# Queries and keys of eight token tiles by seven half products a pair, with low parts and softmax steps moved to Pool

## The chip, the cores and the metric

The kernel runs on one core of a Trainium2 chip. The metric is the device time of one execution, in microseconds. The engines that matter are PE (TensorE), DVE (VectorE), ACT (ScalarE), POOL (GpSimd) and the DMA queues that SP and ACT issue to. Each engine takes its own instructions in order and waits on semaphores for the others.

## The reference

With S = 2048 tokens of width D = 512, 32 heads of 16, and F = 1792:

```python
xn = layernorm(x)                                  # no weights
q, k, v = split_heads(xn @ wqkv)                   # [512, 1536]
kg, vg = k, v at positions s - 2*j, j = 0..7       # dilated sliding window
logits = sum(q * kg, -1) * 16 ** -0.5              # masked where s - 2*j < 0
o = sum(softmax(logits) * vg); s = merge_heads(o) @ wo
h = relu(xn @ w1 + b1) ** 2
g = silu(h @ w2 + b2)
out = x + s * g
```

All is float32.

## The kernel before

**Products.** A float32 factor is kept as a high part (rounded to the matmul's format by an ACT copy, `high`) and a low part (the rest, by a subtraction, `low`), and a product is made of three passes, high by high, high by low and low by high (`PASSES`). A product of 128 tokens by 512 columns with 512 summed over is so 4 slices (kt) by 3 passes, 12 matmuls of 128x512.

**First stage.** The 16 tiles of 128 tokens (t) are taken in pairs a, b = a + 1. For each tile there is a product q, k and v (`qkv(t, s)`, s = 0, 1, 2; `pq` in the profile). Its result lies in one of four PSUM banks (`psA`, tag "acc"), which are taken in turn; ACT copies it to `stg` (`evacuate`), and each pair's stg goes to DRAM (sq, sk, sv), from where attention loads its own layout. In the same stage, ahead by two pairs, a tile is normalised: from tile 6 on ACT sums the row (`mean`, tile scratch) and Pool scales the sum; ACT sums the squares (`spread`) and Pool makes the inverse deviation (`rs`: scale, then power) and `shift`; ACT writes `xn` (`norm`). A pair's xn goes through DMAs (`shuffle`, to `xb`), DVE transposes it (`trans`, to `pxT`), ACT copies the high part (`xt`) and DVE subtracts the low one (`lowx`).

**Second stage.** For four chunks c of 512 tokens, and f = 0 to 13: `up` makes 128 rows of h in PSUM (`ph`), ACT applies relu and squares, DVE subtracts the low part (`lowh`); `down` adds h times w2 into four banks `pb`. The output products of attention (`pw`) are put between them. The weights w1 and w2 are split in the same way (`w`), the first two by DVE, the others by Pool.

**Attention.** 8 units of 256 tokens run on DVE beside all that: four multiplications k by q of 128x2048 (`pr`) with their reductions to L, softmax steps on L (subtract the maximum, exp on ACT, multiply by the inverse sum), four multiplications by v (`pv`) with their reductions.

**What sets the order.** Each engine's instructions stand in the order in which the program's Python issues them: the helper `Ordered` records each one, so most have its line, L80 (L84 in the changed kernel). Only attention is placed by a planner: `pump` draws attention's next step whenever the sum of DVE's estimated durations lies behind PE's. So the order of calls in the loop over pairs is the order of each engine. Names in the order views carry a running number at their end, such as `pq2_0_399`: product 0 (q) of tile 2; `DMA` rows are loads and stores issued by that engine.

## Time and profile before

| | us |
|---|---|
| median of 3 runs | 496.63 (496.25 to 498.05) |
| the profiled execution | 495.58 |
| its span | 493.8 |
| PE busy | 487.5 (99%) |
| DVE busy | 431.7 (87%) |
| ACT busy | 211.0 (43%) |
| POOL busy | 97.9 (20%) |

The span is the stretch that the profiler shows; the execution's own time has 1.78 us more around it. Rows of a timeline read: start and duration in us, engine, line, operation, written tile <- read tiles, how many, and in brackets how long the engine had stood idle, and what released it. Rows of groups give the busy time, the mean duration in ns, and the idle time before them. The windows view gives, for each stretch, the busy time of each engine with its instructions, then the granted clock of PE, the share of the DMA engines and GB/s.

### The profile page before, as it was taken

What the parts mean: (1) busy time and instruction counts of PE and PEld (TensorE: products, weight loads), DVE (VectorE), ACT (ScalarE), POOL (GpSimd) and SP (SyncE); (2) the same over time, 40 slices, a digit from 0 to 9 for tenths busy, and PEclk for the clock granted to TensorE, in tenths of its full rate; (3) what the DMA queues carried; (4) which work ended last, traced back from release to release, by engine and by line L of the source; (5) the groups of instructions that cost most, each with busy time, mean ns of one, the idle gap of its engine ahead of it and who ended that gap; (6) DMA issues with size and microseconds to landing.
All of it is one profiled execution on the core that took longest, in us unless ns stands there. A gap on an engine that the chain in (4) does not pass through costs nothing.

```text
span 493.8 us, 5860 instructions
## 1 busy us (share of the span) xinstructions
PE 487.5 (99%) x2154; PEld 401.1 (81%) x2154; DVE 431.7 (87%) x370; ACT 211.0 (43%) x377; POOL 97.9 (20%) x105
## 2 busy tenths in 40 slices
PE   8999999999999999999999999999999999999997
PEld 5888888888888888887888888888888888888886
DVE  5925798998999999998999998899999889999445
ACT  5636455563343665316333324432252354313331
POOL 1311015571000779300112000112100011220000
PEclk9999999999999999999999999999999999999999
DMA  7999979769977892653406408043241805030222
GB/s 287 297 287 341 304 238 313 225 238 323 372 228 262 203 274 65 202 212 118 127 31 216 181 22 329 4 164 123 85 161 43 328 2 202 1 127 1 85 85 86
DMA packets 48520, 88.79 MB, mean 180 GB/s; under 512 B 5372, under 2 KB 32364, under 8 KB 45676
## 3 DMA queue, kind: packets, MB, share of 16 engines
q1 hardware_dynamic: 44172, 54.87, 35.3%
q10 hardware_dynamic: 4320, 33.56, 19.1%
q8 instruction: 17, 0.28, 0.2%
q14 instruction: 11, 0.09, 0.1%
HBM read 57.94 MB, written 27.32 MB: 173 GB/s over the span
## 4 chain that ended last, share of the span: by engine, by line
PE 83%; DVE 9%; issue 4%; ACT 2%; DMA 1%; ACTq 0%; POOL 0%; DVEq 0%; POOLq 0%
PE pq L80 27%; PE ph L80 24%; PE pb L80 24%; PE pw L80 8%; DVE v L80 2%; DVE pr L80 2%; DVE h L80 2%; DVE pv L80 1%; DMA x<-in_A_x 1%; ACT ph L80 0%; DVE sm_None L80 0%; ACT z L80 0%; DVE z L80 0%; ACT h L80 0%; PE pxT L80 0%
## 5 line engine op out<-in xcount | busy, mean ns | idle before, releaser
L80 PE MATMUL pb<-w,h 128*128 128x512 f32 x672 | 160.6, 389 | 0.0
L80 PEld LDWEIGHTS pb<-w,h 128*128 128x128 f32 x672 | 126.1, 188 | 26.2
L80 PE MATMUL ph<-xU,w 128*128 128x512 f32 x504 | 120.7, 389 | 0.3 <-DVE h L80 0.3
L80 PEld LDWEIGHTS ph<-xU,w 128*128 128x128 f32 x504 | 94.6, 188 | 20.2 <-DVE h L80 0.7
L80 ACT ACTIVATE ph<-ph,b1t 128x512 f32<-128x512 f32 x56 | 37.0, 661 | 163.0 <-PE ph L80 158.4
L80 PE MATMUL pq<-wq,xt 128*128 128x512 f32 x432 | 98.7, 390 | 0.0
L80 PEld LDWEIGHTS pq<-wq,xt 128*128 128x128 f32 x432 | 81.0, 188 | 17.2 <-ACT stg L80 0.3
L80 DVE TENSOR_TENSOR pr<-k,q 128x2048 f32<-128x2048 f32 x32 | 75.4, 2356 | 0.3
L80 DVE TENSOR_TENSOR pv<-v,L 128x2048 f32<-128x2048 f32 x32 | 73.8, 2305 | 0.4
L80 DVE TENSOR_REDUCE L<-pr 128x128 f32<-128x2048 f32 x32 | 72.9, 2279 | 0.6
L80 DVE TENSOR_REDUCE v<-pv 128x256 f32<-128x2048 f32 x32 | 72.9, 2279 | 0.6
L80 POOL TENSOR_TENSOR z<-z,xr 128x512 f32<-128x512 f32 x12 | 23.2, 1936 | 214.7 <-DVE z L80 209.9
L80 DVE TENSOR_TENSOR h<-ph,h 128x512 fp32r<-128x512 f32 x56 | 38.3, 683 | 19.9 <-ACT ph L80 19.9
L80 PE MATMUL pw<-wot,oT 128*128 128x512 f32 (+1 forms) x204 | 45.9, 376 | 0.0
L80 PEld LDWEIGHTS pw<-wot,oT 128*128 128x128 f32 x204 | 36.8, 188 | 7.1
L80 PE MATMUL ph<-xT,w 128*128 128x512 f32 x168 | 40.7, 391 | 0.0
L80 ACT ACTIVATE stg<-pq 128x512 f32<-128x512 f32 x48 | 27.2, 595 | 26.4 <-PE pq L80 16.9
L80 PEld LDWEIGHTS ph<-xT,w 128*128 128x128 f32 x168 | 31.5, 188 | 7.0 <-DVE h L80 0.4
L80 ACT ACTIVATE h<-ph 128x512 fp32r<-128x512 f32 x56 | 33.7, 601 | 1.8
L80 ACT ACTIVATE ph<-ph 128x512 f32<-128x512 f32 x56 | 33.3, 595 | 0.0
L80 PE MATMUL pq<-wq,xT 128*128 128x512 f32 x132 | 31.7, 398 | 0.0
L80 POOL TENSOR_TENSOR w<-w1r,w 128x512 fp32r<-128x512 f32 x12 | 18.9, 1577 | 57.1 <-DMA rwo<-in_A_wo 48.8
(66 smaller groups left out, 309.9 us busy)
## 6 DMA issues: line engine op xcount, KB each, us to landing
k<-sk ACTq DMA_DIRECT2D x8, 1408.0 KB, 8.1
v<-sv ACTq DMA_DIRECT2D x8, 1408.0 KB, 8.3
sx<-xt SPq DMA_DIRECT2D x12, 512.0 KB, 5.5
xU<-sx ACTq DMA_DIRECT2D x6, 1024.0 KB, 5.4
x<-in_A_x SPq DMA_DIRECT2D x16, 256.0 KB, 5.0
sk<-stg SPq DMA_DIRECT2D x8, 512.0 KB, 7.1
sq<-stg SPq DMA_DIRECT2D x8, 512.0 KB, 5.6
q<-sq ACTq DMA_DIRECT2D x8, 512.0 KB, 8.4
```

The costliest lines, as they stand in the source:

```text
L80: return tc.keep_in_program_order(f(*a, **k))
```

## The change

**Seven half products.** For the pairs 4, 6, 8 and 10, q and k of the two tiles are one 2 by 2 block product: the blocks are the two tiles by the two halves of the 512 summed over, and q and k by the same halves. `pair_of_seven` makes it from seven products of 6 matmuls (`pm<a>_<n>`) in place of four of 12, a form of Strassen's scheme: some factors are sums. Four sums of weight halves (T1 to T4) replace the raw weights at the start of the pairs (DVE in place, ACT the high and Pool the low parts, into `wq6` to `wq9`). Four sums of transposed x, 128 by 256 each (`Sf`, highs and lows in `S<a>_0`, `S<a>_1`), are made in each pair for the next (`sums`, `low_sums`); the low part of `S<a>_1` is Pool's. ACT copies the products 1 and 5, DVE adds the other five to the half-made results in `stg`, and Pool makes two more additions. v stays as it was.

**Places of the normalisation.** `mean`, `spread` and `norm` of a pair start half a pair earlier: mean(a + 6) and spread(a + 6) stand around v of tile a + 1, and the first norm stands at the start of the next pair.

**Weights.** wq lies in ten buffers; the later w buffers w1 to w10 take their places as they come free (`HOME`). The loads and splits of w come later: w0 is split at the end of pair 4, w1 and w2 at the end of pair 12, w3 and w4 at the end of pair 14, then one in each of the first chunk's steps; Pool makes all their low parts.

**Softmax.** For the units 1 to 7 the subtraction of the maximum and the multiplication by the inverse sum are Pool's. The factor 0.25 moves from q's copy into the exponential.

**Low part of h.** From the second chunk on ACT writes the full square to SBUF (`hf`, one buffer) and Pool subtracts.

```diff
+SEVEN = range(4, 12, 2)
...
-            V.tensor_sub(L, L, mx[:, :, None].to_broadcast([P, n, W]))
+            (G if h is None else V).tensor_sub(L, L, mx[:, :, None].to_broadcast([P, n, W]))
...
-                A.activation(L, L, AF.Exp)
+                A.activation(L, L, AF.Exp, scale=0.25)
...
-            V.tensor_mul(L, L, sm[:, :, None].to_broadcast([P, n, W]))
+            (G if h is None else V).tensor_mul(L, L, sm[:, :, None].to_broadcast([P, n, W]))
...
+    def next_w():
+        f = len(w12)
+        if f < NF:
+            w12[f] = buffer(f"w{f}", HOME[f]) if f in HOME else p2.tile([P, 2, 2, 512], FR, name=f"w{f}")
+            for i, r in enumerate(raws.pop(f)):
+                split(w12[f][:, 0, i], w12[f][:, 1, i], r, G)
+            if f + 2 < NF:
+                load_w(f + 2)
...
+    def sums(a, half):
+        (pa, pb), n = (pTs[t].rearrange("p (h m) -> p h m", h=2) for t in (a, a + 1)), 2 * half
+        if half == 0:
+            Sf[a] = hpool.tile([P, 4, 2 * P], F32, name=f"Sf{a}", tag="h", bufs=3)
+            A.activation(Sf[a][:, 3], pb[:, 0], AF.Copy)
+            not_before(seen[a + 1])
+            V.tensor_add(Sf[a][:, 0], Sf[a][:, 3], pb[:, 1])
+            V.tensor_sub(Sf[a][:, 1], Sf[a][:, 0], pa[:, 0])
+        else:
+            V.tensor_sub(Sf[a][:, 2], pa[:, 0], Sf[a][:, 3])
+            V.tensor_sub(Sf[a][:, 3], pa[:, 1], Sf[a][:, 1])
+        Sp[a, half] = hpool.tile([P, 2, 2, 2, P], FR, name=f"S{a}_{half}", tag="h", bufs=3)
...
+        A.activation(Sp[a, half][:, 0].rearrange("p j k n -> p (j k n)"),
+                     Sf[a][:, n:n + 2].rearrange("p j m -> p (j m)"), AF.Copy)
+    def low_sums(a, half, eng):
...
+        eng.tensor_sub(Sp[a, half][:, 1].rearrange("p j k n -> p (j k n)"),
+                       Sf[a][:, n:n + 2].rearrange("p j m -> p (j m)"),
+                       Sp[a, half][:, 0].rearrange("p j k n -> p (j k n)").bitcast(F32))
...
+    def product(a, n, lhs, w):
+        ps = psA(f"pm{a}_{n}")
+        k = 0
+        for i in range(2):
+            for p, q in PASSES:
+                PE.matmul(ps, lhs(p, i), wq[w][:, q, i, :], start=k == 0, stop=k == 5)
+                k += 1
...
-        A.activation(ph, ph, AF.Square)
+        full = hpool.tile([P, 512], F32, name=f"hf{c}_{f}", tag="hf") if c else ph
+        A.activation(full, ph, AF.Square)
+        if c:
+            G.tensor_sub(h[:, 1], full, h[:, 0].bitcast(F32))
...
     shuffle(4)
-    split_w(0, V)
+    for d, x0, x1 in (((0, 0), (1, 0), (0, 0)), ((1, 0), (1, 2), (1, 0)),
+                      ((1, 2), (1, 2), (0, 0)), ((0, 2), (0, 2), (1, 2))):
+        for i in range(2):
+            V.tensor_sub(*(raws[s, kt + i] for s, kt in (d, x0, x1)))
+    for w, (s, kt) in ((T1, (0, 0)), (T2, (1, 2)), (T3, (1, 0)), (T4, (0, 2))):
+        for i in range(2):
+            split(wq[w][:, 0, i], wq[w][:, 1, i], raws[s, kt + i], G)
     pump(LATE)
+    mean(6)
     qkv(1, 2)
-    split_w(1, V)
+    spread(6)
+    mean(7)
     pump(LATE)
...
+    def pair_of_seven(a):
...
+        if ahead:
+            norm(a + 4)
+            spread(b + 4)
+        p = product(a, 1, part_x(a, 0), Q0)
+        A.activation(q[:, :, 0], p, AF.Copy)
+        p = product(a, 5, part_s(a, 0), T1)
+        A.activation(k[:, :, 1], p, AF.Copy)
+        pump(LATE)
+        if ahead:
+            norm(b + 4)
+            shuffle(a + 4)
+        p = product(a, 6, part_s(a, 1), T2)
+        not_before(clock["PE"])
+        V.tensor_add(k[:, :, 0], q[:, :, 0], p)
+        p = product(a, 2, part_x(a, 1), Q1)
+        pump(LATE)
+        not_before(clock["PE"])
+        V.tensor_add(q[:, :, 0], q[:, :, 0], p)
+        p = product(a, 7, part_s(a, 2), T3)
+        pump(0)
+        not_before(clock["PE"])
+        V.tensor_add(q[:, :, 1], k[:, :, 0], p)
+        G.tensor_add(k[:, :, 0], k[:, :, 0], k[:, :, 1])
+        G.tensor_add(k[:, :, 1], k[:, :, 1], q[:, :, 1])
+        qkv(a, 2)
+        trans(a + 2)
+        trans(b + 2)
+        if seven:
+            sums(a + 2, 0)
+        pump(LATE)
+        p = product(a, 3, part_s(a, 3), K1)
+        lowx(a + 2)
+        pump(LATE)
+        not_before(clock["PE"])
+        V.tensor_add(k[:, :, 0], k[:, :, 0], p)
+        store_qkv(b, 1)
+        p = product(a, 4, part_x(b, 1), T4)
+        if seven:
+            low_sums(a + 2, 0, V)
+            sums(a + 2, 1)
+        pump(LATE)
+        not_before(clock["PE"])
+        V.tensor_add(q[:, :, 1], q[:, :, 1], p)
+        store_qkv(b, 0)
+        lowx(b + 2)
+        if seven:
+            low_sums(a + 2, 1, G)
...
+    NEXT = {4: 1, 12: 2, 14: 2}
+    for a in range(2, NT, 2):
...
+        (pair_of_seven if a in SEVEN else pair)(a)
+        if a == 2:
+            load_w(0)
+            load_w(1)
+        for n in range(NEXT.get(a, 0)):
+            next_w()
+        if a + 6 < NT:
+            mean(a + 6)
+        pump(LATE)
+        qkv(a + 1, 2)
+        if a + 6 < NT:
+            spread(a + 6)
+            mean(a + 7)
```

**Where instructions move.** POOL at the start of the pairs, before (the powers of tiles 4 and 5, then tiles 6 and 7):

```order
L80 TENSOR_TENSOR rs4_329<-rs4_329,mhalf_136 128x1
L80 TENSOR_TENSOR rs5_336<-rs5_336,mhalf_136 128x1
L80 TENSOR_SCALAR mean6_395<-mean6_395 128x1
L80 TENSOR_SCALAR rs6_414<-rs6_414 128x1
L80 TENSOR_TENSOR rs6_414<-rs6_414,mhalf_136 128x1
L80 TENSOR_TENSOR shift6_415<-mean6_395,rs6_414 128x1
L80 TENSOR_SCALAR mean7_421<-mean7_421 128x1
```

and in the changed kernel, where `wq6` to `wq9` hold T1 to T4:

```order
L84 TENSOR_TENSOR rs4_326<-rs4_326,mhalf_143 128x1
L84 TENSOR_TENSOR rs5_333<-rs5_333,mhalf_143 128x1
L84 TENSOR_TENSOR wq6_117<-wqraw0_133,wq6_117 128x512 x2
L84 TENSOR_TENSOR wq7_118<-wqraw1_2_129,wq7_118 128x512
L84 TENSOR_TENSOR wq7_118<-wqraw1_3_131,wq7_118 128x512
L84 TENSOR_TENSOR wq8_119<-wqraw1_0_123,wq8_119 128x512
L84 TENSOR_TENSOR wq8_119<-wqraw1_1_127,wq8_119 128x512
L84 TENSOR_TENSOR wq9_120<-wqraw0_133,wq9_120 128x512 x2
L84 TENSOR_SCALAR mean6_390<-mean6_390 128x1
L84 TENSOR_SCALAR rs6_409<-rs6_409 128x1
L84 TENSOR_TENSOR rs6_409<-rs6_409,mhalf_143 128x1
L84 TENSOR_TENSOR shift6_410<-mean6_390,rs6_409 128x1
```

The eight low parts of the combined weights stand between the powers of tiles 4 and 5 and the mean of tile 6.

ACT around the copy of q of tile 2 (`stg2_0<-pq2_0`), before:

```order
L80 ACTIVATE scratch6_396,mean6_395<-x6_236 128x512
L80 ACTIVATE stg2_0_412<-pq2_0_399 128x4x128
L80 ACTIVATE scratch6_416,rs6_414<-x6_236,mean6_395 128x512
L80 ACTIVATE scratch7_422,mean7_421<-x7_297 128x512
L80 ACTIVATE stg2_0_412<-pq3_0_425 128x4x128
L80 ACTIVATE xt4_440<-pxT4_441 128x512
L80 ACTIVATE xn6_444<-x6_236,shift6_415,rs6_414 128x4x4x32
L80 ACTIVATE scratch7_450,rs7_448<-x7_297,mean7_421 128x512
L80 ACTIVATE stg2_1_468<-pq2_1_455 128x4x128
```

and changed:

```order
L84 ACTIVATE scratch6_391,mean6_390<-x6_243 128x512
L84 ACTIVATE stg0_2_350<-pq1_2_394 128x4x128
L84 ACTIVATE scratch6_411,rs6_409<-x6_243,mean6_390 128x512
L84 ACTIVATE scratch7_417,mean7_416<-x7_294 128x512
L84 DMA q0_420<-sq_147 128x1x1024
L84 ACTIVATE xn6_423<-x6_243,shift6_410,rs6_409 128x4x4x32
L84 ACTIVATE scratch7_429,rs7_427<-x7_294,mean7_416 128x512
L84 ACTIVATE stg2_0_447<-pq2_0_434 128x4x128
L84 ACTIVATE xn6_423<-x7_294,shift7_428,rs7_427 128x4x4x32
L84 ACTIVATE stg2_0_447<-pq3_0_457 128x4x128
```

The copy of q of tile 2 stood behind the first sum of tile 6; now it stands behind the squares of tiles 6 and 7 and the first norm, and the copy of q of tile 3 behind the second norm.

PE in pair 6, before:

```order
L80 MATMUL pq6_0_684<-wq0_111,xt6_579 128x512 x12
L80 MATMUL pq7_0_713<-wq0_111,xt7_612 128x512 x12
L80 MATMUL pq6_1_748<-wq1_112,xt6_579 128x512 x12
L80 MATMUL pq7_1_776<-wq1_112,xt7_612 128x512 x12
L80 MATMUL pq6_2_805<-wq2_113,xt6_579 128x512 x12
L80 MATMUL pq7_2_824<-wq2_113,xt7_612 128x512 x12
```

and changed, up to the first product of pair 8:

```order
L84 MATMUL pm6_1_756<-wq0_111,xt6_662 128x512 x6
L84 MATMUL pm6_5_764<-wq6_117,S6_0_674 128x512 x6
L84 MATMUL pm6_6_782<-wq7_118,S6_0_674 128x512 x6
L84 MATMUL pm6_2_790<-wq1_112,xt6_662 128x512 x6
L84 MATMUL pm6_7_799<-wq8_119,S6_1_696 128x512 x6
L84 MATMUL pq6_2_809<-wq4_115,xt6_662 128x512 x6
L84 MATMUL pq6_2_809<-wq5_116,xt6_662 128x512 x6
L84 MATMUL pm6_3_838<-wq3_114,S6_1_696 128x512 x6
L84 MATMUL pm6_4_848<-wq9_120,xt7_666 128x512 x6
L84 MATMUL pq7_2_868<-wq4_115,xt7_666 128x512 x6
L84 MATMUL pq7_2_868<-wq5_116,xt7_666 128x512 x6
L84 MATMUL pm8_1_911<-wq0_111,xt8_824 128x512 x6
```

Four products of q and k have become seven of 6 matmuls; the products 1, 5, 6 and 2 stand ahead of product 7, and v of tile 6 stands between 7 and 3. In the changed kernel a whole product is shown as two rows of 6.

More of the change, by code (lines that the diff above doesn't have):

```diff
@@ L119, in split @@
         low(hi, lo, src, eng)
-    ident = const.tile([P, P], F32, name="ident")
+    p1ctx = ExitStack()
+    px, pstg, pxT = (p1ctx.enter_context(tc.tile_pool(name=n, bufs=1)) for n in ("px", "pstg", "pxT"))
+    xins = {}
+    ident = px.tile([P, P], F32, name="ident")
     make_identity(nc, ident)
@@ L138, in load_x, with buffer @@
         dma(xins[t], tile_rows(x, t))
-    wq = [pwq.tile([P, 2, KT, 512], FR, name=f"wq{s}") for s in range(3)]
+    def buffer(name, i):
+        return wts.tile([P, 2, 2, 512], FR, name=name, tag=f"b{i}")
+    wq = [buffer(f"wq{i}", i) for i in range(10)]
     raws = {}
@@ L564, in body @@
     constants()
-    for f in range(2):
-        load_w(keep, f)
     qkv(0, 0, lambda: highs(2, 0))
@@ L642, in body @@
         if a == NT - 4:
             dma(b1t, b1.rearrange("(f p) -> p f", p=P))
[L644 to L647 removed]
+        pump(LATE if a + 2 < NT else -SLACK)
     lowh(1)
```

145 lines of the change are left out of this document (69 added, 76 removed).

## The prediction

> **What bounds the kernel now.** I read the page first: the busy table and the chain that ended last.
>
> ```profile
> span 493.8 us, 5860 instructions
> PE 487.5 (99%) x2154; PEld 401.1 (81%) x2154; DVE 431.7 (87%) x370; ACT 211.0 (43%) x377; POOL 97.9 (20%) x105
> PE 83%; DVE 9%; issue 4%; ACT 2%; DMA 1%; ACTq 0%; POOL 0%; DVEq 0%; POOLq 0%
> ```
>
> PE is busy 99% of the span, and its products are the chain. Next, the chain's pieces in order of time, and the idle columns of the groups:
>
> ```profile
> 20.12 112.45 PE pq L80 x492
> 470.92 5.44 PE pw L80 x24
> L80 PE MATMUL pq<-wq,xt 128*128 128x512 f32 x432 | 98.7, 390 | 0.0
> L80 ACT ACTIVATE stg<-pq 128x512 f32<-128x512 f32 x48 | 27.2, 595 | 26.4 <-PE pq L80 16.9 <-DVE L L80 8.2 <-DMA xb<-xn 1.4
> ```
>
> In the q, k, v stage PE runs 492 matmuls without a gap: 112.45/492 = 0.2286 us each, 2.743 us for a product of 12. It never waited for a copy out of PSUM, although ACT, which makes those copies in its program order, sometimes stood for a long time. Four banks hide it: a product may be copied up to three products late, 3 x 2.743 = 8.23 us after its end. ACT, around 30 to 40 us (start, duration, instruction, idle before):
>
> ```profile
> 28.59 0.60 ACT L80 ACTIVATE stg<-pq 128x512 f32<-128x512 f32 x1 [0.56 <-PE pq L80]
> ...
> 29.69 0.20 ACT L80 ACTIVATION_READ_ACCUMULATOR scratch<-x,mean 128x1 f32 x1
> ...
> 31.40 0.60 ACT L80 ACTIVATE stg<-pq 128x512 f32<-128x512 f32 x1 [0.76 <-PE pq L80]
> 38.14 0.60 ACT L80 ACTIVATE xt<-pxT 128x512 fp32r<-128x512 f32 x1 [6.14 <-DVE pxT L80]
> 38.63 0.81 ACT L80 ACTIVATE xn<-x,shift,rs 128x512 f32<-128x512 f32 x1
> 39.34 0.71 ACT L80 ACTIVATE scratch<-x,mean 128x512 f32<-128x512 f32 x1
> 39.95 0.19 ACT L80 ACTIVATION_READ_ACCUMULATOR scratch<-x,mean 128x1 f32 x1
> 40.05 0.58 ACT L80 ACTIVATE stg<-pq 128x512 f32<-128x512 f32 x1
> ```
>
> The copy at 40.05 is of k of tile 2, which PE had ended at 33.84 (20.12 + 5 x 2.743); it stood behind a transpose that ACT waited 6.14 us for, and cost nothing, since its bank was wanted at 42.07. So the question is whether the changed orders stay inside that slack.
>
> **The gain.** Each of the four pairs takes 42 matmuls for q and k instead of 48: 24 x 0.2286 = 5.5 us, the only work that leaves PE. A pair becomes 66 matmuls, 15.09 us, instead of 72, 16.46 us. But the new products are of 6 matmuls, 1.37 us, and three of them give a copy only 4.1 us of slack instead of 8.2.
>
> **The first wait: the combined weights on Pool.** Eight DVE differences, eight ACT highs and eight Pool lows now stand ahead of tile 6's mean on Pool; behind that mean, on ACT, stand the spreads of tiles 6 and 7, tile 6's norm, and behind them the copy of q of tile 2. That copy frees the bank for v of tile 2, due to start at 20.12 + 6 x 2.743 = 36.58. The rows of now:
>
> ```profile
> 24.90 0.69 DVE L80 TENSOR_TENSOR w<-w1r,w 128x512 fp32r<-128x512 f32 x1
> 25.50 0.69 DVE L80 TENSOR_TENSOR w<-w2r,w 128x512 fp32r<-128x512 f32 x1
> ...
> 28.11 0.23 POOL L80 TENSOR_SCALAR mean<-mean 128x1 f32<-128x1 f32 x1 [3.71 <-ACT scratch L80]
> 29.97 0.19 POOL L80 TENSOR_SCALAR rs<-rs 128x1 f32<-128x1 f32 x1 [1.63 <-ACT scratch L80]
> 30.24 0.57 POOL L80 TENSOR_TENSOR rs<-rs,mhalf 128x1 f32<-128x1 f32 x1
> 30.89 0.19 POOL L80 TENSOR_TENSOR shift<-mean,rs 128x1 f32<-128x1 f32 x1
> ```
>
> The differences start where DVE split w0 before, 24.90, 0.61 us apart. One difference (to 25.6) and one high (0.62) put the first low at 26.3. What a low costs on Pool:
>
> ```profile
> 94.69 1.29 POOL L80 TENSOR_TENSOR w<-w1r,w 128x512 fp32r<-128x512 f32 x1 [1.93 <-ACT w L80]
> 94.89 3.24 DVE L80 TENSOR_TENSOR pr<-k,q 128x2048 f32<-128x2048 f32 x1
> 95.94 3.35 POOL L80 TENSOR_TENSOR w<-w2r,w 128x512 fp32r<-128x512 f32 x1
> 98.17 2.29 DVE L80 TENSOR_REDUCE L<-pr 128x128 f32<-128x2048 f32 x1
> 100.49 2.29 DVE L80 TENSOR_TENSOR pr<-k,q 128x2048 f32<-128x2048 f32 x1
> 100.69 2.53 POOL L80 TENSOR_TENSOR rs<-rs,mhalf 128x1 f32<-128x1 f32 x1
> ```
>
> A low alone takes 1.25 (94.69 to 95.94). The next one lay under DVE's big multiplication and took 3.35: it ended 1.16 after that did. The multiplication itself was 0.95 over its usual 2.29, about as long as the first low still had to run. Likewise a power of 128x1, 0.57 alone, took 2.53. So a Pool operation and a DVE operation of two SBUF inputs run one after the other, either way. The differences are such operations. Eight lows: 26.3 + 8 x 1.25 = 36.4; with some 5.6 differences still to come, x 0.61 = 3.4: 39.8. Behind them mean 0.2, spread 0.9 with its read, rs, power and shift 1.2 (29.97 to 31.08), norm 0.71 and spread 0.71 (38.63 to 40.05), copy 0.6: 44.2. Waited: 44.2 - 36.58 = **7.6 us**; without the turns 4.2. [...]
>
> **Pair 4.** Its sums of transposed halves follow in a row. From PE's resuming at s: the end of tile 7's power chain on Pool 0.65, norm 0.71, two copies 1.1, four steps of transposing and splitting tile 4 and 5 (0.6 to 0.7 each) 2.55, a half copy and two sums of 128x256 1.25, high and low of the first sums 1.3, two differences and a high 1.5: s + 9.0 in all, some of it overlapping, I take 8.5. Then Pool's low of the second sums 1.25, and tile 8's mean, spread, rs with power and shift (a power under DVE's first multiplication, +0.7), norm, the spread of tile 9, and the copy of product 1: 0.25 + 0.95 + 1.85 + 0.75 + 0.7 + 0.6 = 5.1, so s + 15.0. PE wants that bank for product 7, the fifth in its order, after 48 matmuls, s + 10.97: **4.0 us** (3.3 without turns). For the small pieces the nearest row is this, with the transposes and the splits:
>
> ```profile
> 490.15 0.42 DVE L80 TENSOR_TENSOR z<-z,pw 128x256 f32<-128x256 f32 x1 [0.48 <-PE pw L80]
> ...
> L80 DVE STREAM_TRANSPOSE pxT<-xb 128x512 f32<-128x512 f32 x12 | 8.6, 718 | 18.6 <-DMA xb<-xn 18.6
> L80 DVE TENSOR_TENSOR xt<-pxT,xt 128x512 fp32r<-128x512 f32 x12 | 8.2, 680 | 2.4 <-ACT xt L80 2.4
> ```
>
> **Pairs 6, 8, 10.** From here each pair is a ring of waits from one copy of product 1 to the next. DVE's add to k's first half 0.7, the multiplication's reduction that stands next in DVE's order 2.25, two adds 1.2, both transposes and ACT's half copy 2.35, two sums 0.9, split, add and the first low 1.9, two differences 0.8, ACT's high 0.65, Pool's low 1.3, mean 0.25, spread 0.95, rs to shift 1.15, norm 0.8, spread 0.7, copy 0.55: 16.45 us, against PE's 15.09. In pair 6 w0's two lows stand on Pool ahead of tile 10's mean, +2.5, and one of them meets a DVE multiplication, +2.3: 21.25, a wait of **6.2**. Pair 8: a power under a multiplication, +2.1: 18.55, **3.5**. Pair 10: a softmax step on DVE in the ring, +0.85: 17.3, **2.2**. Without turns 3.9, 1.4 and 1.4; if every handover is 0.1 shorter than I took it, pairs 8 and 10 wait for nothing.
>
> **What I take at nothing.** Low parts of h, softmax steps, and the w buffers:
>
> ```profile
> L80 DVE TENSOR_TENSOR h<-ph,h 128x512 fp32r<-128x512 f32 x56 | 38.3, 683 | 19.9 <-ACT ph L80 19.9
> L80 POOL TENSOR_TENSOR z<-z,xr 128x512 f32<-128x512 f32 x12 | 23.2, 1936 | 214.7 <-DVE z L80 209.9
> L80 DVE TENSOR_TENSOR L<-L,mx_None 128x512 f32<-128x512 f32 x7 | 5.7, 812 | 0.2
> L80 DVE TENSOR_TENSOR L<-L,sm_None 128x512 f32<-128x512 f32 x7 | 5.6, 800 | 0.2
> 261.48 2.72 PE ph L80 x12
> 458.26 2.28 DVE L80 TENSOR_REDUCE v<-pv 128x256 f32<-128x2048 f32 x1
> 467.33 0.69 DVE L80 TENSOR_TENSOR h<-ph,h 128x512 fp32r<-128x512 f32 x1 [4.75 <-ACT ph L80]
> ```
>
> DVE loses 42 x 0.683 = 28.7 and 7 x 1.61 = 11.3 us, 40.0. Its order shows the attention 9 big multiplications with their reductions behind at the end of the first chunk (17 and 12 done there before, now 12 and 8), 9 x 4.6 = 41 by the rows above. So it ends about where it did, 460.5 plus the stalls, while the last out products at 470.92 move by the same stalls: 10 us of cover, taken at 0. A low of h on Pool takes 1.3 to 3.4 and is wanted two steps, four products of 2.72 or 10.9 us, later: 0, at worst 4 if the one full-square buffer holds ACT once or twice. The later w loads in the first chunk wait behind Pool's split two steps ahead: 0, up to 1.7. The q scale moved into the exponential adds no instruction.
>
> **Sum.** The profiled run took 495.58, of which 493.8 is the span: 495.58 - 5.5 + 7.6 + 4.0 + 6.2 + 3.5 + 2.2 = 513.6. The median of the runs shown, 496.63, is 1.05 above the profiled one: 514.6, say 514.5.
>
> **Rivals.**
> *The turns do not count here.* Then the waits are 4.2 + 3.3 + 3.9 + 1.4 + 1.4 = 14.2, and the time 505. For it: my rows show 128x2048 multiplications against Pool, none a 128x512 difference. Against it: a 128x1 power was held as long.
> *The other side: the banks take it all up.* If ACT's copies come in time everywhere, all of the gain stays: 495.58 - 5.5 + 1.05 = 491.1, faster. The place is Pool's mean of tile 6: it must be done by 36.58 - 4.2 = 32.4, which asks that eight lows take 6.1 us, 0.76 each. For it: PE has never waited for a copy in this stage. Against it: no low in the rows is under 1.25.
> *About even.* Only the first wait without turns, 4.2, the later rings just inside PE's pace: 495.58 - 5.5 + 4.2 + 1.05 = 495.3.
> *PE's clock falls in the gaps.* The last slice shows that the granted clock can fall when PE stands:
>
> ```profile
> 490.00:492.00 2.00, 0.11 (x1) 0.00 (x0) 0.84 (x2) 0.00 (x0) 0.00 (x0) 1.00 0.40 140
> 492.00:493.80 1.80, 0.00 (x0) 0.00 (x0) 0.00 (x0) 0.00 (x0) 0.00 (x0) 0.56 0.17 56
> ```
>
> If a product ran at 0.56 after a gap, 2.743 us would be 4.90: 2.15 more. In the rings the copy of product 1 would not come later for it, so the next wait would be shorter by as much; only the last gap's 2.15 is left, 516.7. Where DVE's adds wait for the slower products the ring grows too: up to three gaps more, 2.15 each, 523. Against it: the row falls where the program ends. [...]
>
> **How the numbers follow.** Forecast 0.58 (its own range 507 to 520), no turns 0.13, lower clock 0.10, other side 0.12, about even 0.07. The predicted time is the forecast's, 514.5. The range leaves out the other side and the even case, 0.19: from 498 (the first two waits at their low ends, 7.5, and none later: 498.6) to 522 (the lower clock, most of its gaps not taken up). A measurement of this kernel tells about 0.5% from no change: faster is the other side, 0.12; within 0.5% the even case, 0.07; slower the rest, 0.81.
>
> **What would show it.** Right: PE idle before v of tile 2 at about 36.6, for 4 to 8 us, released by ACT's stg; on Pool eight lows from 26 to 36 or 40 and then the mean; in the four pairs of seven, PE idle ahead of product 7, once a pair, largest in pair 6; no idle time of PE after 140 that was not there. Wrong: PE unbroken from 20 to 127, or lows well under 1.25; or new waits in the chunks, on the full-square buffer or the w loads, or in the attention's end.

## The result

The changed kernel takes 524.37 us (median of 4 runs, 523.89 to 525.79), the kernel before beside it 497.34: a ratio of 1.0549, with a 95% interval of 1.0515 to 1.0583. It is slower, as forecast, but by 27 us where 17 were forecast, and above the end of the range (522).

The page of the changed kernel, busy times, granted clock and chain:

```profile
span 522.1 us, 5929 instructions
PE 492.6 (94%) x2130; PEld 401.6 (77%) x2130; DVE 429.6 (82%) x358; ACT 217.9 (42%) x389; POOL 213.7 (41%) x185
PEclk9996997998999999999999999999999999999999
PE 65%; POOL 10%; issue 10%; ACT 5%; DVE 5%; DMA 3%; SPq 0%; POOLq 0%; ACTq 0%; DVEq 0%
```

PE has 24 matmuls less and yet is busy 5.1 us longer, and it now stands still for 6% of the span; Pool is in the chain with 10%. PEclk shows three dips early in the span. PE's waits, in all, times and the longest:

```profile
PE pm L84 <- ACT stg L84: 13.0, 4, 5.2
PE pq L84 <- ACT stg L84: 7.5, 1, 7.5
PE ph L84 <- DVE h L84: 3.4, 3, 1.7
```

Where they are, from PE's timeline:

```profile
43.91 8.33 PE L84 MATMUL pq<-wq,xT 128*128 128x512 f32 x24 [7.50 <-ACT stg L84]
...
60.01 1.66 PE L84 MATMUL pm<-wq,S 128*128 128x512 f32 x6 [2.20 <-ACT stg L84]
...
80.84 2.93 PE L84 MATMUL pm<-wq,S 128*128 128x512 f32 x6 [5.23 <-ACT stg L84]
83.57 4.50 PE L84 MATMUL pq<-wq,xt 128*128 128x512 f32 x12
...
102.06 1.66 PE L84 MATMUL pm<-wq,S 128*128 128x512 f32 x6 [2.83 <-ACT stg L84]
...
120.42 2.36 PE L84 MATMUL pm<-wq,S 128*128 128x512 f32 x6 [2.73 <-ACT stg L84]
...
129.06 28.16 PE L84 MATMUL pq<-wq,xt 128*128 128x512 f32 x120
157.06 2.93 PE L84 MATMUL ph<-xT,w 128*128 128x512 f32 x12
```

The five waits stand where the prediction put them: ahead of v of tile 2, and ahead of product 7 of each pair, all released by ACT's copy to stg. Behind three of them the rows are too long for their matmuls: 24 in 8.17 us (43.91 to the next product at 52.08), where the 120 undisturbed ones take 28.0, 0.2333 each, which would be 5.6. The windows of the changed kernel (busy times of PE, PEld, DVE, ACT and POOL, then PE's granted clock) show why:

```profile
36.00:38.00 2.00, 0.41 (x2) 0.00 (x0) 0.00 (x0) 0.00 (x0) 2.00 (x2) 1.00 0.74 215
38.00:40.00 2.00, 0.00 (x0) 0.00 (x0) 0.00 (x0) 0.17 (x1) 1.79 (x3) 0.80 1.01 268
40.00:42.00 2.00, 0.00 (x0) 0.00 (x0) 0.00 (x0) 1.50 (x5) 1.12 (x4) 0.50 0.54 190
...
48.00:50.00 2.00, 2.00 (x7) 1.59 (x6) 0.84 (x2) 1.06 (x3) 0.00 (x0) 0.64 1.09 181
50.00:52.00 2.00, 2.00 (x10) 1.65 (x9) 1.71 (x4) 1.04 (x3) 0.00 (x0) 1.00 1.11 342
```

The granted clock falls to half in the gap (at 39.2: a share of (1 - 0.80)/0.5 of the second window is low) and is back only at 49.4, five microseconds after PE resumes. The same happens in pair 6 and pair 10; the windows of all three are in the last section.

The pitch, the time from one matmul's start to the next, changed too. Rows of PE in the first stage, before and changed:

```profile
19.87 22.73 PE L80 MATMUL pq<-wq,xT 128*128 128x512 f32 x96
42.44 90.13 PE L80 MATMUL pq<-wq,xt 128*128 128x512 f32 x396
132.41 2.94 PE L80 MATMUL ph<-xT,w 128*128 128x512 f32 x12
...
19.82 16.59 PE L84 MATMUL pq<-wq,xT 128*128 128x512 f32 x72
```

A row's length holds some 0.16 us more than its matmuls' pitch, because the next product starts that much before the last matmul ends (129.06 + 28.16 = 157.22, and the next starts at 157.06). From start to start, the matmuls of tiles 0 to 3 (`xT`) took 22.57/96 = 0.2351 us each before and 16.43/72 = 0.2282 in the changed kernel; those of the later tiles (`xt`) took 89.97/396 = 0.2272 before and 0.2333 now. So the 0.2286 of the prediction is a mean of two pitches, and the two have changed places.

The whole, by PE's end (490.11 before, 518.38 after, +28.3):

| term | forecast | measured |
|---|---|---|
| 24 matmuls fewer, x 0.2286 | -5.5 | -5.5 |
| five waits | +23.5 (7.6, 4.0, 6.2, 3.5, 2.2) | +20.5 (7.5, 2.2, 5.2, 2.8, 2.7) |
| half clock behind three of them | 0 | +7.1 (2.6, 2.9, 1.6) |
| waits for h (3.4, all in the first chunk; 0.3 before) | 0 | +3.1 |
| pitch: shorter for tiles 0 to 3, longer for the later ones, together | 0 | +2.0 |
| overlap of two products lost at each wait, 0.16 x (8 waits - 1 before) | 0 | +1.1 |

### The profile page after: what moved, and what is told of

Its sections match the earlier page's. It is cut to its first block, busy times and chain, and to the rows that moved or that the text cites. A ratio compares the mean times of both kernels' runs of the same rounds, so it can differ in the third digit from the quotient of the medians.

```text
span 522.1 us, 5929 instructions
## 1 busy us (share of the span) xinstructions
PE 492.6 (94%) x2130; PEld 401.6 (77%) x2130; DVE 429.6 (82%) x358; ACT 217.9 (42%) x389; POOL 213.7 (41%) x185
## 4 chain that ended last, share of the span: by engine, by line
PE 65%; POOL 10%; issue 10%; ACT 5%; DVE 5%; DMA 3%; SPq 0%; POOLq 0%; ACTq 0%; DVEq 0%
PE pb L84 26%; PE ph L84 25%; PE pw L84 8%; PE pq L84 4%; POOL w L84 3%; POOL wq L84 2%; POOL rs L84 2%; ACT scratch L84 1%; POOL S L84 1%; PE pm L84 1%; DMA w2r<-in_B_w 1%; DVE pr L84 1%; DVE Sf L84 1%; DMA sv<-stg 1%; ACT stg L84 1%
## 5 line engine op out<-in xcount | busy, mean ns | idle before, releaser
L84 POOL TENSOR_TENSOR h<-hf,h 128x512 fp32r<-128x512 f32 x42 | 66.9, 1593 | 154.7 <-ACT hf L84 143.8
L84 DVE TENSOR_TENSOR pv<-v,L 128x2048 f32<-128x2048 f32 x32 | 77.2, 2414 | 6.3 <-POOL L L84 5.8
L84 DVE TENSOR_TENSOR pr<-k,q 128x2048 f32<-128x2048 f32 x32 | 80.2, 2507 | 0.5
L84 PE MATMUL pq<-wq,xt 128*128 128x512 f32 x240 | 60.0, 407 | 0.0
L84 PEld LDWEIGHTS pq<-wq,xt 128*128 128x128 f32 x240 | 47.2, 197 | 11.7
L84 PE MATMUL ph<-xT,w 128*128 128x512 f32 x168 | 40.9, 392 | 3.4 <-DVE h L84 3.4
L84 POOL TENSOR_TENSOR w<-w1r,w 128x512 fp32r<-128x512 f32 x14 | 27.6, 1969 | 33.6 <-ACT w L84 33.6
L84 PE MATMUL pq<-wq,xT 128*128 128x512 f32 x132 | 33.7, 416 | 7.5 <-ACT stg L84 7.5
L84 PE MATMUL pm<-wq,S 128*128 128x512 f32 x96 | 26.5, 422 | 13.0 <-ACT stg L84 13.0
L84 PEld LDWEIGHTS pq<-wq,xT 128*128 128x128 f32 x132 | 26.3, 202 | 14.3 <-ACT stg L84 7.9
L84 ACT ACTIVATE stg<-pq 128x512 f32<-128x512 f32 x32 | 19.0, 593 | 43.6 <-PE pq L84 41.6
```

The lines of the kernel that those rows point to most:

```text
L84: return tc.keep_in_program_order(f(*a, **k))
```

## The experiments

The median of the kernel before lay between 497.3 and 499.3 us from one set of runs to the next, so kernels are compared by their ratios to the kernel before beside them: 1.0549 is the change. The changed kernel was not run again beside its edits. By the plain medians most of the gains below are 1 to 3 us smaller than by the ratios, and a difference of that size is not shown.

### The lows of the combined weights on DVE

```diff
-            split(wq[w][:, 0, i], wq[w][:, 1, i], raws[s, kt + i], G)
+            split(wq[w][:, 0, i], wq[w][:, 1, i], raws[s, kt + i], V)
```

> The eight low parts of the combined weights are made by DVE instead of Pool; nothing else differs from the change. My theory (Pool's order holds tile 6's mean behind the eight lows): the mean runs near 32 instead of 39.5, the copy of q of tile 2 ends near 36.2 instead of 43.9, PE's first gap of 7.5 us goes, and with it the low clock after it (2.7 us of PE's time); the wait of pair 4 grows from 2.2 to up to 4, since PE comes there earlier. Time about 516 (514 to 519). Rival, ACT's own order of sums and norms holds the copy: the gap stays over 3 us and the time over 520.

Measured: 1.0383 (1.0350 to 1.0415), 8.3 us less than the change (5.6 by the medians). The first gap falls from 7.5 to 2.37 and no low clock follows it; pair 4's wait grows from 2.2 to 4.4 in two pieces. So the lows on Pool were the cause, and the rival falls. That 2.37 was left has its own reason; POOL of this kernel:

```profile
32.13 2.67 POOL L84 TENSOR_SCALAR mean<-mean 128x1 f32<-128x1 f32 x1 [7.64 <-ACT scratch L84]
```

and DVE:

```profile
29.80 4.90 DVE L84 TENSOR_TENSOR wq<-wqraw,wq 128x512 fp32r<-128x512 f32 x8
```

A mean of 128x1 that took 0.23 before takes 2.67: it ends at 34.80, when DVE's run of eight subtractions ends (34.70). In the change it was the lows that were shut out; DVE:

```profile
24.84 4.90 DVE L84 TENSOR_TENSOR wqraw<-wqraw,wqraw 128x512 f32<-128x512 f32 x8
```

and POOL:

```profile
26.27 13.31 POOL L84 TENSOR_TENSOR wq<-wqraw,wq 128x512 fp32r<-128x512 f32 x8 [1.93 <-ACT wq L84]
39.52 0.28 POOL L84 TENSOR_SCALAR mean<-mean 128x1 f32<-128x1 f32 x1
```

Eight lows take 13.31, 3.3 more than 8 x 1.25: the first of them took 4.63, from 26.27 to 30.90, and DVE's eight differences were through at 29.74. This is the term with turns of the prediction (mean after 39.8, measured 39.52).

### The copies of products 1 and 5 first

```diff
-        if ahead:
-            norm(a + 4)
-            spread(b + 4)
         p = product(a, 1, part_x(a, 0), Q0)
         A.activation(q[:, :, 0], p, AF.Copy)
         p = product(a, 5, part_s(a, 0), T1)
         A.activation(k[:, :, 1], p, AF.Copy)
+        if ahead:
+            norm(a + 4)
+            spread(b + 4)
```

> In the pairs of seven the ACT copies of products 1 and 5 stand ahead of the norm and the spread instead of behind them; nothing else differs from the change. My theory (each pair is a ring through ACT's order): about 2.1 to 2.6 us leave each ring; the wait at product 7 falls from 2.2, 5.2, 2.8, 2.7 to about 0, 3, 0.5 and 0.5; the first gap of 7.5 stays. Time about 514 (511 to 518). Rival, the norms that now come later hold the shuffled x back: DVE's transposes wait for it and the gaps only move: 521 or more.

Measured: 1.0240 (1.0210 to 1.0271), 15 us less than the change (12.9 by the medians; 511.5, near the fast end of what was said). The waits at product 7 are 0.46, 3.24, none and 0.79. The ring of waits through ACT's order is real, and cutting one link, with the clock that no longer falls in pair 10, is worth more than any other single edit here. The first gap did not stay as it was: it came as 1.41 and 5.33, the last section says why.

### w0 later

```diff
-    NEXT = {4: 1, 12: 2, 14: 2}
+    NEXT = {10: 1, 12: 2, 14: 2}
```

> The split of w0 stands at the end of pair 10 instead of pair 4; nothing else differs from the change. My theory (w0's two lows on Pool lengthen the ring of pair 6, and the low clock after that gap lengthens the ring of pair 8): pair 6 waits under 1.5 us instead of 5.2 and no low clock follows; the distance between products 7 falls from 20.8 to about 16.2 and from 21.2 to about 18.5. Time about 517 (515 to 519). Rival, the gaps add up without the ring and the clock: only 3.7 goes, 520.7. Rival, w0 is not the cause: no change.

Measured: 1.0438 (1.0400 to 1.0476), 5.5 us less by the ratio, between the theory and its first rival; the median, 521.30, is the rival's. Pair 6's wait is 2.75 instead of 5.23, not under 1.5. Its ring, expected at 16.2, measures 19.9 (59.65 to 79.56). With w0 gone, the next Pool instruction met the same DVE multiplication:

```profile
71.90 1.29 POOL L84 TENSOR_TENSOR S<-Sf,S 128x512 fp32r<-128x512 f32 x1 [5.39 <-ACT S L84]
73.17 2.26 POOL L84 TENSOR_SCALAR mean<-mean 128x1 f32<-128x1 f32 x1
```

The mean takes 2.26 instead of 0.23. In the change, too, one Pool instruction of each pair of seven was about 2 us longer than the others of its kind: the low of the second sums in pair 4 (3.20, 1.29 in pair 6), w0's first low in pair 6 (3.35), the scale of rs in pair 8 (2.15 instead of 0.19), the mean in pair 10 (2.27). So w0's own lows leave this ring, the 2 us of being shut out do not. Another 1.5 us of the 19.9 come from the clock, which in this run was low for 3.4 us behind the wait of pair 4. The second half of the theory held: no low clock follows pair 6, and the next ring, 21.2 in the change, is 18.45 (79.56 to 98.01). But the clock fell behind the waits of the pairs 8 and 10 instead, 1.6 us each, so little of the time came back.

### Filling the gaps

```diff
+    def idle(n):
+        if n:
+            ps = psH("idle")
+            for i in range(n):
+                tc.keep_in_program_order(nc.tensor.matmul(ps, xt[2][:, 0, 0], wq[4][:, 0, 0, :], start=i == 0, stop=i == n - 1))
...
+        if a == 2:
+            idle(24)
         qkv(a, 2)
...
+        idle({4: 8, 6: 14, 8: 6, 10: 6}[a])
         p = product(a, 7, part_s(a, 2), T3)
```

> Products whose result nobody reads fill PE's gaps: 24 matmuls ahead of v of tile 2, and 8, 14, 6 and 6 ahead of product 7 of the pairs 4, 6, 8 and 10; nothing else differs from the change. This prices the low clock after a gap. Theory, partly absorbed by the next wait: the granted clock stays at 1.00 from 20 to 130, the gaps (with the filling) become about 7.5, 4, 5.2, 2.8 and 2.7, the distance of products 7 of pairs 6 and 8 falls from 21.2 to about 18.5; time about 519 (517.5 to 520.5). Rival, nothing is absorbed: all 7.65 us of slow matmuls come off, 516.7 or less. Rival, all is absorbed: 522 to 524.

Measured: 1.0443 (1.0400 to 1.0486), 5 us less by the ratio, the size of the first theory, and 2.6 by the medians; its time alone decides nothing. The profiled execution was the slowest of its four (523.90, the others 519.51 to 522.39), and in it the clock no longer fell behind the first gap and pair 10, but it did behind the waits of pairs 4 and 6, where 2.15 and 2.04 us were left unfilled. The trace does tell which part is absorbed. From v of tile 2 to product 7 of pair 4 it takes 16.12 us (43.38 to 59.50) at full clock, and 16.10 in the change (43.91 to 60.01), where the first half of the way ran at half clock: the clock behind the first gap costs nothing, the wait of pair 4 takes it up. The rings behind pair 4 and pair 6, with 3.4 us of low clock each, measure 22.43 and 19.99, the last one, at full clock, 18.36. What the low clock does to a ring is told in the account of the prediction.

### No product of seven

```diff
-SEVEN = range(4, 12, 2)
+SEVEN = ()
...
-    for d, x0, x1 in (((0, 0), (1, 0), (0, 0)), ((1, 0), (1, 2), (1, 0)),
...
-            split(wq[w][:, 0, i], wq[w][:, 1, i], raws[s, kt + i], G)
```

> All pairs by the old four products of 12 matmuls; the combined weights and the sums are left out. The rest of the change stays (places of the normalisation, ten weight buffers, later loads, softmax steps and low parts of h on Pool). My theory: the four waits of the pairs of seven, the first gap and the low clock all come from the seven products and their preparation, so PE runs the stage from 20 to 145 without a gap and at clock 1.00; 24 matmuls, 5.5 us, come back; the first chunk's three waits of 3.4 us stay. Time 500 to 503 where the kernel before takes 497 to 499. Rival, the moved normalisation itself makes waits: gaps at the start of pairs stay, 506 or more. The matmul's pitch in this stage tells a side question: 0.2286 as before, or 0.2333 as in the change; if 0.2333, the ten buffers or their places have to do with it, if 0.2286, the seven products and their sums.

Measured: 1.0096 (1.0070 to 1.0121), 502.71 us. Four fifths of the loss belong to the seven products and their preparation: with 5.5 us of matmuls more, the kernel is 22 us faster than the change. One gap of 2.31 at v of tile 2 stays, and 1.9 of waits in the first chunk. The gap has about the size of the one left in the first experiment, but another reason. Pool's mean of tile 6 runs at 25.20 here, and it is ACT's norm of tile 6 that comes late, ACT of this kernel:

```profile
36.83 0.81 ACT L84 ACTIVATE xn<-x,shift,rs 128x512 f32<-128x512 f32 x1 [9.05 <-DMA xb<-xn]
```

The norm writes the one buffer from which the pair before is shuffled, and the shuffle, issued at 25.51, has only just landed. So the moved normalisation has a part in the loss too. The side question: the stage's pitch is long here as well. A view of PE's timeline, this kernel:

```profile
44.47 92.56 PE L84 MATMUL pq<-wq,xt 128*128 128x512 f32 x396
```

The next product starts at 136.86: 92.39/396 = 0.2333 us each, against 0.2272 before. So the pitch is not the seven products'.

### The w splits behind the relu

```diff
-            if c == 0:
-                next_w()
             up(c, f)
+            if c == 0:
+                next_w()
             pump()
```

> In the first chunk's steps the split of the next w stands behind the step's up product and its relu, instead of ahead of it; nothing else differs from the change. My theory (ACT's highs of w wait for the late load and hold the relu behind them): PE's three waits of 3.4 us in the first chunk fall under 0.6. Time about 521.5 (520.5 to 522.5). Rival, DVE's attention step in front of the low part of h holds PE: the waits stay, 524.

Measured: 1.0507 (1.0478 to 1.0536), 2 us less (0.3 by the medians), which the intervals do not tell from nothing. PE's waits in the first chunk are 2.9 in two instead of 3.4 in three, so the theory holds for one of them. In the change these two rows of ACT stand in front of the waits at 183.21 and 201.57:

```profile
179.39 0.63 ACT L84 ACTIVATE w<-w1r 128x512 fp32r<-128x512 f32 x1 [7.60 <-DMA w1r<-in_B_w]
...
197.41 0.52 ACTq L84 DMA_DIRECT2D v<-sv  x1
```

The first is the high of w that waited for its load, with the relu behind it; this wait went. The second is ACT's issue of the load of attention's v. Here, its row and the next on ACT:

```profile
198.56 0.52 ACTq L84 DMA_DIRECT2D v<-sv  x1
199.19 0.66 ACT L84 ACTIVATE ph<-ph,b1t 128x512 f32<-128x512 f32 x1 [6.84 <-DMA so<-v]
```

The load goes into a buffer whose store (so<-v) has not landed, and the relu stands behind it for 6.84 us. That the store is late because DVE's attention is late is likely, but not shown here.

### The low parts of h back on DVE

```diff
-        full = hpool.tile([P, 512], F32, name=f"hf{c}_{f}", tag="hf") if c else ph
-        A.activation(full, ph, AF.Square)
-        if c:
-            G.tensor_sub(h[:, 1], full, h[:, 0].bitcast(F32))
-        hs[f] = h, None if c else ph, clock["PE"] + 2000
+        A.activation(ph, ph, AF.Square)
+        hs[f] = h, ph, clock["PE"] + 2000
```

> The low parts of h of the chunks 1 to 3 are DVE's again, as before; nothing else differs from the change. My theory (the seven pairs cost DVE what Pool's relief gives back): DVE's last attention reduction ends about 20 to 29 us later than its 491.7, past the last out products at 499, and PE waits for it: time 534 to 545. Rival, DVE has enough room and the move to Pool is worth nothing: within 1 us of the change.

Measured: 1.1369 (1.1346 to 1.1393), 566.5 us, worse than expected. Attention's last reduction ends at 542.7, 51 us later than in the change, and PE waits for DVE in every chunk:

```profile
PE ph L84 <- DVE h L84: 21.0, 10, 6.9
...
PE pb L84 <- DVE h L84: 9.0, 1, 9.0
```

The move to Pool is needed once the seven products have taken DVE's time: 29 us of subtractions decide over 41.

### Four edits together

The edits of the lows, the copies, w0 and the relu, as above.

> Four edits together: the low parts of the combined weights on DVE, the copies of products 1 and 5 ahead of the norm, w0's split at the end of pair 10, the w splits of the first chunk behind the relu. My theory, by the runs so far: the first gap 2.4, pair 4 about 1, the other pairs under 1 each, the first chunk under 0.6, no low clock; of the 28.3 us lost some 24 come back: 499 to 502 against 499 of the kernel before on the same chip, within 0.6% of it. Rival, the waits only move to where one of these edits uncovers the next thing late: 508 or more.

Measured: 1.0083 (1.0060 to 1.0106): 23 us come back, about as expected; 502.12 lies just past the end of what was said. PE's waits in the pairs are 1.18, 0.75, none and 0.75. Two things were not as said: the first gap of 2.35 still brought a stretch of low clock, which cost 1.6 us (24 matmuls in 7.20, 40.71 to 47.91, instead of 5.6), and the first chunk kept 2.1 us of waits.

### Toward a faster one

In the next kernels DVE's batch-norm instructions make the statistics and norms of tiles 6 and 7 (STATS 8), beside the four edits; the further edits are these:

```diff
-            low_sums(a + 2, 1, G)
+            low_sums(a + 2, 1, V)
...
-BEHIND, FREE, LAND, LOAD = 5000, 2000, 6000, 11500
+BEHIND, FREE, LAND, LOAD = 5000, 6000, 6000, 11500
```

> The four edits of the run before, and the statistics and norms of tiles 6 and 7 by DVE's batch-norm instructions instead of ACT and Pool. My theory (the first gap of 2.35 us that was left came from Pool's mean standing shut out behind DVE's unbroken run of lows, and ACT's order behind it): that gap goes, and the low clock behind it (some 2 us); pair 4 waits about 1. Time 0.8% less than the four edits alone, 497 to 499 where the kernel before takes 498. Rival, the next copies in ACT's order hold the same banks: a gap over 1.5 us stays.

> As the run with the statistics on DVE, and two more edits: the low part of the second sums on DVE instead of Pool, and loads of the attention's tiles planned 4 us later. My theory: Pool's low (1.3) leaves the ring, so product 7 waits under 0.3 in the pairs 6 to 10; ACT no longer stands at the load of v for the store before it, so the first chunk's waits of 1.6 and 0.5 go. Time 2 to 4 us under the run before it, 494 to 496 where the kernel before takes 498: ratio 0.992 to 0.998. Rival, the later loads make DVE's attention late and it ends after the last products ask for it: 499 or more.

Measured: 1.0124 (1.0084 to 1.0165) with the statistics alone, 1.0097 (1.0061 to 1.0134) with all. The first gap is gone, but each kernel has a new one: 3.18 and 2.44 us in pair 4, where ACT and DVE wait for `DMA sq<-stg`, and 7.11 and 2.85 in the first chunk, ACT again behind `DMA so<-v`. Both expectations fail: the waits moved.

> The kernel before, for its trace on the chip of this call. If the matmul's pitch in the first stage is 0.2333 here too, the longer pitch belongs to the chip or the execution, not to the change; if it is 0.2286, to the change. Time 497 to 499.5.

Measured: 498.06, in one execution, with 0.2350 us a matmul for tiles 0 to 3 (96 from 19.89 to 42.45) and 0.2279 for later ones (168 from 95.73 to 134.01). So the exchange of the two pitches is the change's. The kernel before had 2.0 us of waits in this execution.

The store that pair 4 waited for stood on SP behind the shuffle of tiles 6 and 7; here it goes first, and v's loads alone are planned later:

```diff
             norm(b + 4)
+        qkv(b, 0)
+        if ahead:
             shuffle(a + 4)
-        qkv(b, 0)
...
-                defer(max(clock["V"] + FREE if u else 0, done_tiles[n][1][u] + LAND), start)
+                defer(max(clock["V"] + (12000 if n == "v" else FREE) if u else 0, done_tiles[n][1][u] + LAND), start)
```

> As the run with statistics on DVE (lows of the combined weights on DVE, copies of products 1 and 5 first, w0 later, w splits behind the relu), and three edits for what its trace and the next showed late: the low part of the second sums on DVE; the store of pair 2's q issued ahead of the shuffle of tiles 6 and 7 on SP; the loads of attention's v planned 10 us later, those of q and k as in the change. My theory: PE's wait of 2.4 to 3.2 us in pair 4 (for the stg buffer that this store frees) goes, and the first chunk's wait of 2.9 to 7.1 (ACT at the load of v, which waits for the store of the unit before) falls under 1. PE loses under 2.5 us in all from 20 to 240; time 492 to 496 where the kernel before takes 498: ratio 0.988 to 0.996. Rival, v then comes late for DVE and attention ends late: waits at the end, 499 or more.

Measured: 1.0105 (1.0087 to 1.0123). PE loses only 2.8 us between 20 and 490, and then the rival's wait comes, PE's timeline:

```profile
490.39 8.30 PE L84 MATMUL pw<-wot,oT 128*128 128x512 f32 x36 [6.28 <-DVE oT L84]
```

Attention's last reduction ends at 480.6. The store, the load and the transposes behind it take until 490.39, and the last three output products were due at 484.1.

> The kernel before with the raw query, key and value weights in six buffers of two slices instead of three of four, and nothing else. If the split of the weights into more buffers makes the matmul's pitch of the first stage longer, it is 0.233 here and the time 1.5 to 2.5 us over the kernel before; if it does not, 0.2286 and the same time.

Measured: 0.9999 (0.9974 to 1.0024), with 0.2351 us a matmul for tiles 0 to 3 and 0.2277 later, as before. The split of the weights into smaller buffers is not what makes the later tiles' pitch longer.

The last two, with 6000 and 8000 in place of 12000, the second with the low of the second sums on DVE:

> As the run with the earlier store of q, but the low part of the second sums stays on Pool, and v's loads are planned 4 us later instead of 10. It tells what the late end of attention in that run came from. Theory, v's loads came too late for DVE: attention ends before the last out products, the first chunk's wait is 0 to 3, the pairs wait under 1.5 in all; 494 to 498 where the kernel before takes 498.5: ratio 0.991 to 0.999. Rival, DVE simply has too much work once PE waits no longer (the seven products cost it some 27 us): attention is late again and PE waits at the end, 500 or more.

> As the run beside it, with v's loads planned 6 us later and the low part of the second sums on DVE (2.7 us more of DVE's time). By the theory of late loads 494 to 498; by the rival of DVE's work 1 to 3 us more than the run beside it.

Measured: 1.0064 (1.0038 to 1.0090) and 1.0007 (0.9986 to 1.0027), 501.84 and 498.44 us. Attention's last reduction ends at 469.4 and 471.6, in time for its products in both. The second differs from the run before by the plan of v's loads alone, so the loads planned 10 us later made attention late, not DVE's whole work. Both times miss the 494 to 498 that were said, the second by 0.4. In the first, PE still waits 5.26 us in the first chunk, where ACT stands 7.63 us at v's load behind `DMA so<-v`, and the 12 matmuls behind that wait take 4.95 us (178.00 to 182.95), 2.72 in the rows after them. The second one's waits of PE:

```profile
PE ph L84 <- DVE h L84: 3.2, 4, 1.0
PE pm L84 <- ACT stg L84: 1.4, 3, 0.7
```

So all of the 27 us can be taken back, and the 5.5 us of the scheme still do not show: 4.6 us of small waits (2.0 in the single execution of the kernel before) and some 2 us of pitch take most of them. No kernel here beats the one before.

## Why the prediction was wrong

**The direction and the mechanism were right.** The first wait came where it was said, by the chain that was said, at its size (7.6, measured 7.5), and the run with the lows on DVE takes it away. The four waits at product 7 were right in place, with the largest in pair 6; at full clock they would have been right in sum as well (below).

**The steps that failed.** First, the sum took a falling clock at nothing, and the rival of the clock was priced at 2.15 after the last gap, because "the next wait would be shorter by as much". The clock stays low not for one product but for 10.2, 6.8 and 3.4 us from its fall, and takes 2.6, 2.9 and 1.6 us from PE. Only pair 4 shortened its wait for it (4.0 forecast, 2.2 measured; 4.4 where the clock did not fall ahead of it). Behind pair 6 it lengthened the next ring instead: the slow product there is v, whose copy stands on ACT ahead of the copies of x that the sums need. DVE's rows of the change, in pairs 6 and 8, and of the run with w0 later, in the same pairs:

```profile
90.05 0.88 DVE L84 TENSOR_TENSOR Sf<-Sf,pxT 128x256 f32<-128x256 f32 x2 [3.92 <-ACT Sf L84]
108.50 0.88 DVE L84 TENSOR_TENSOR Sf<-Sf,pxT 128x256 f32<-128x256 f32 x2 [1.15 <-ACT Sf L84]
...
85.99 0.88 DVE L84 TENSOR_TENSOR Sf<-Sf,pxT 128x256 f32<-128x256 f32 x2 [1.15 <-ACT Sf L84]
105.99 0.88 DVE L84 TENSOR_TENSOR Sf<-Sf,pxT 128x256 f32<-128x256 f32 x2 [2.70 <-ACT Sf L84]
```

DVE waits 1.15 where v runs at full clock, 2.70 where the clock was low for 3.4 us behind the wait, and 3.92 where it was low for 6.8. The rings, from one product 7 to the next, follow:

| ring | what lies in it | us |
|---|---|---|
| pair 8 to 10, change | full clock | 18.36 |
| pair 6 to 8, w0 later | full clock | 18.45 |
| pair 8 to 10, w0 later | low for 3.4 us | 19.90 |
| pair 6 to 8, change | low for 6.8 us | 21.22 |
| pair 4 to 6, change | w0's lows, full clock | 20.83 |
| pair 4 to 6, lows on DVE | w0's lows, low for 3.4 us | 22.39 |

So a ring is 18.4 us at full clock, w0 adds 2.4, and a low clock adds 1.5 or 2.8, about what it takes from PE. The wait behind such a ring is not shorter for it: pair 8 waits 2.83 in the change and 2.84 with w0 later. Of the 7.1 us of low clock, then, the 2.6 behind the first gap cost nothing (from v of tile 2 to product 7 of pair 4 it takes 16.10 us with it, and 16.11 without in the run with the lows on DVE), and the 4.5 behind pairs 6 and 10 are lost. The prediction had named the growth ("Where DVE's adds wait for the slower products the ring grows too") within a rival of a tenth of the chance. It is the largest part of the 10.3 us that were missed (28.3 measured, 18.0 forecast).

Second, the first chunk was taken at nothing: "0, up to 1.7". The late loads of w were named, the load of v was not: its issue on ACT waits for its buffer, and the work behind it on ACT waits too (the relu 6.84 us, in the run with the w splits behind it). Together 3.4.

Third, a term was missing: the pitch of the first stage, 2.0 us, the sum of some -0.6 for tiles 0 to 3 (0.2351 to 0.2282) and +2.6 for the later ones (0.2272 to 0.2333). Its cause is open. It is there without any product of seven and not there with the weights in six buffers; the other moves of that stage were not tried one by one. The overlap lost at each wait, 1.1 in all, was not counted either.

**What was wrong the other way.** The rings were forecast at 21.25, 18.55 and 17.3 and measured at 20.8, 21.2 and 18.4; pair 4's wait at 4.0 was 2.2. Of the waits' sum 3.0 us too much was taken; 2.6 of that is the low clock that pair 4's wait took up, so at full clock the waits' sum was right to within a microsecond. That is partly luck: pair 6 was forecast 1.0 too long and pair 10 0.5 too short. In the rival without turns, pair 10 was put at 1.4, but its softmax step is no turn: by its own terms it is 2.2, and that rival's time 506.

**Taken at nothing, and rightly so:** the low parts of h on Pool from the second chunk on (no wait of PE from 240 to the end), the softmax steps for PE, and the end of attention.

**The rivals.** Without turns: refuted, the first of Pool's lows took 4.63 beside DVE's run, the others some 1.3 behind it. The other side and the even case: refuted with the first gap. The lower clock: it came, inside the program and beside the forecast, not in its place.

## What to carry to other kernels

Halving a product's length halves the time that its copy may be late (here from 8.2 to 4.1 us, an estimate from the pitch), so with a ring of four banks a scheme with fewer matmuls needs copies that stand first in their engine's order; count the links of the ring of waits before the matmuls saved. Put no run of DVE subtractions beside small Pool instructions on which an in-order chain hangs (beside eight of them, 4.90 us, a mean of 0.23 us took 2.67). And price a gap of PE with the low clock that may come behind it: in the change the gaps of 7.5, 5.23 and 2.73 us were followed by 2.6, 2.9 and 1.6 us of slower matmuls, those of 2.20 and 2.83 by none, and the loss was taken up only where the next wait did not itself hang on the slow products.

## What the runs showed of the hardware

**The granted clock fell and came back in steps of 3.41 us.** The changed kernel's windows at its three falls and returns:

```profile
38.00:40.00 2.00, 0.00 (x0) 0.00 (x0) 0.00 (x0) 0.17 (x1) 1.79 (x3) 0.80 1.01 268
48.00:50.00 2.00, 2.00 (x7) 1.59 (x6) 0.84 (x2) 1.06 (x3) 0.00 (x0) 0.64 1.09 181
80.00:82.00 2.00, 1.16 (x3) 0.97 (x4) 1.18 (x2) 1.73 (x5) 0.95 (x3) 0.54 0.95 363
86.00:88.00 2.00, 2.00 (x8) 1.55 (x8) 0.13 (x1) 0.00 (x0) 1.59 (x2) 0.76 0.41 75
120.00:122.00 2.00, 1.58 (x5) 1.30 (x6) 1.60 (x2) 1.66 (x3) 0.92 (x3) 0.78 0.00 0
124.00:126.00 2.00, 2.00 (x9) 1.62 (x8) 2.00 (x4) 0.00 (x0) 1.32 (x2) 0.87 1.02 164
```

By the share of half clock in each, it falls at 39.2, 80.2 and 121.1 and returns at 49.4, 87.0 and 124.5: low for 10.2, 6.8 and 3.4 us, and from fall to fall 41.0 and 40.9. All of these lie within 0.1 of multiples of 3.41 us (3, 2, 1, 12 and 12). Three other runs, read in the same way, show the same:

| run | falls | low for | from fall to fall, in steps of 3.41 |
|---|---|---|---|
| lows on DVE | 55.4, 75.8, 99.8 | 3.4, 6.8, 3.4 | 20.5 (6), 23.9 (7) |
| copies first | 41.7, 75.8 | 6.8, 6.8 | 34.1 (10) |
| w0 later | 43.6, 60.6, 98.2, 118.7 | 3.4, 3.4, 3.4, 3.4 | 17.1 (5), 37.6 (11), 20.5 (6) |

Counted in such steps from the falls of the change (an estimate from these readings), the gap of 2.73 in pair 10 lies wholly in the step from 117.7 to 121.1, and the clock falls at its end; the gap of 2.83 in pair 8 is cut at 100.6 into 1.4 and 1.4, and nothing happens; that of 2.20 in pair 4 gives 1.9 to one step, and nothing happens either. In the run with the lows on DVE a fall came behind 1.93 in one step (pair 8), in the one with w0 later none behind 1.92 (the first gap's beginning): with some 1.9 both were seen. In the change the clock came back at the end of the first step that PE ran almost through: behind pair 6 the step from 80.2, in which PE still stood for 0.7, did not bring it back, the next one did.

**DVE's run and Pool's instructions held each other up, either way.** Beside DVE's eight instructions in a row Pool's low took 3.3 us longer in the change (4.63 instead of 1.29), and its mean 2.4 us longer in the run with the lows on DVE (2.67 instead of 0.23). In the run with the copies first two lows came between and the same eight took 8.21 instead of 4.90, DVE's and Pool's rows:

```profile
24.86 8.21 DVE L84 TENSOR_TENSOR wqraw<-wqraw,wqraw 128x512 f32<-128x512 f32 x8
26.29 3.31 POOL L84 TENSOR_TENSOR wq<-wqraw,wq 128x512 fp32r<-128x512 f32 x2 [1.93 <-ACT wq L84]
```

The eight lost 3.31 us, the time of the two lows. ACT's highs, its sum for tile 6 and the copy behind them then came later too, so the first gap has two pieces, 1.41 and 5.33. The program was the same up to there in both, so its order alone did not decide which of the two was held up.
